# Reordering the first seven microseconds of a fused SSM and GEGLU kernel: tile 0 ahead of tile 1 through LayerNorm, other load requests, dummy matmuls between transposes

## Chip, cores and metric

One NeuronCore of a Trainium2 chip. The metric is the device time of one execution in microseconds, the median of several runs. Positions inside an execution are counted from the start of the profiled span, which is about 1.8 us shorter than the device time.

## The reference, cut to what matters

The input x is 2048 tokens of 512 features in bf16. It is normalised, and two branches read the result: a diagonal complex state-space layer (A) and a GEGLU feed-forward (B).

```python
def reference(A_x, ...):
    x = A_x
    xn = _layernorm(x, axis=-1)
    return x + _A_ref(xn, A_Lambda_re, A_Lambda_im, A_B_re, A_B_im, A_C_re, A_C_im, A_log_dt, A_Dskip) \
             + _B_ref(xn, B_w_gate, B_w_up, B_w_down)

def _B_ref(x, w_gate, w_up, w_down):
    return (_gelu(x @ w_gate) * (x @ w_up)) @ w_down      # 512 -> 1376 -> 512

def _A_ref(x, Lambda_re, Lambda_im, ..., log_dt, Dskip):  # cut
    dt = jnp.exp(log_dt)
    Lam_bar = jnp.exp(dt * (Lambda_re + 1j * Lambda_im))  # h = Lam_bar * h + Bu, token after token
    ...
```

Three small inputs of 1 KB each, `log_dt`, `Lambda_re` and `Lambda_im`, decide the recurrence.

## The kernel before

The kernel records each operation with its reads and writes; a scheduler of its own orders those of VectorE (DVE), ScalarE (ACT) and GpSimd (POOL) and gives every cross-engine dependence a semaphore. TensorE (PE) and the sync queue run in the order in which the program records them. The tokens are cut into 4 blocks of 4 tiles of 128. Per block the matmuls are gate and up (GU), Bu of the state-space branch (BU) and the output (DN). What starts the kernel, cut:

```python
# loads: sync queue, but w_gate's first chunk and the parameters on ScalarE's queue
for j in range(4):
    ld_x0(j)                                                  # tile j of block 0, 128 KB each
ld_w(WG, WGc, ins["B_w_gate"], 0, "scalar").nb = 900.0        # first 384 columns; nb: not before, in the scheduler's model
ld_w(WU, WUc, ins["B_w_up"], 0)                               # ... then chunks 1 of w_gate and w_up
for q, nm in enumerate(("A_log_dt", "A_Lambda_re", "A_Lambda_im")):
    S.dma(lambda e, q=q, nm=nm: e.dma_start(PROW.ap[4 * q:4 * q + 4, :], ins[nm]...), 1024, ..., queue="scalar")
# then on the sync queue: block 1 of x, transposing loads of B_re and B_im, more weights (load_B)

def params():                          # all three parameters, transposed by one small matmul
    PE(f, 100, PROWq + [IDN], [BANK[bank]], "Tpar")           # waits for all three loads
    ...                                # the tables of sines follow from it on POOL, DVE and ACT

def LN(b, js, on_act):                 # cut: statistics and aggregate per tile, then ONE root and reciprocal for all js
    ...
def GU_first(fts, early, banks):       # block 0, in PE's order (early = row blocks 0 to 2)
    for n in (1, 0):                   # tile 0's gate half, by halves of its transpose
        for ft in early: mm(ft, 0, 0, 1, [2 * n, 2 * n + 1], 2, 1, [XT0h[n]])
    for ft in early: mm(ft, 1, 0, 1)   # tile 0's up half
    params()                           # <-- the small transpose stands HERE in PE's order
    for ft in early:
        for u in range(2): mm(ft, u, 1, 2)                    # tile 1's gate and up
    ...                                # the rest: tiles 0 and 1, then the transposes of tiles 2 and 3, then tiles 2 and 3

PE(fwarm, ...)                         # 11 dummy matmuls of 512 columns
LN(0, [0, 1], True)
TR0(0, "AV"); TR0(1, "V", ...)         # PE transposes; copies of tile 0 half on ACT, half on DVE
LN(0, [2, 3], True, ...)
load_B()
GU_first(range(5), range(3), hbanks)
```

Of the kernel before, what the change touches and what calls it, by code (L numbers as in the profile page):

```python
# [15 lines left out]
SELF_LAT = 40.0  # L16
LAT = lambda d, op: SYNC_LAT if d.kind == "dma" or d.eng != op.eng else (0.0 if d.eng == "tensor" else SELF_LAT)
DMA_ISSUE = 500.0
# [43 lines left out]
class Op:  # L62
    __slots__ = ("id", "eng", "fn", "dur", "deps", "kind", "reads", "writes", "start", "finish",
                 "sem", "val", "users", "tag", "issue", "nb")

    def __init__(self, id_, eng, fn, dur, kind, reads, writes, tag):
        self.id, self.eng, self.fn, self.dur, self.kind = id_, eng, fn, float(dur), kind
        self.reads, self.writes, self.tag = reads, writes, tag
        self.deps, self.users = [], []
        self.start = self.finish = None  # L70
        self.sem = None
        self.val = None
        self.issue = DMA_ISSUE
        self.nb = 0.0


class Sched:
# [43 lines left out]
    def dma(self, fn, nbytes, reads=(), writes=(), tag="", after=(), is_output=False, queue="sync", issue=DMA_ISSUE):  # L121
        op = self._add(queue, fn, 2000.0 + nbytes / 0.30e3, "dma", reads, writes, tag, after)
        op.issue = issue
        if is_output:
            self.out_ops.append(op)
        return op

# [84 lines left out]
    def _forward(self, prio):  # L212
# [16 lines left out]
        while nleft:  # L229
# [36 lines left out]
            if op.kind == "dma":  # L266
                free_at[e] = st + op.issue
                xfer = op.dur - 2000.0
                t0 = max(st, dma_pipe)
                dma_pipe = t0 + xfer  # L270
                op.finish = t0 + xfer + 2000.0
            else:
                op.finish = st + op.dur
                free_at[e] = op.finish
# [8 lines left out]
    def emit(self):  # L283
# [19 lines left out]
        for e in ENGINES:  # L303
            seen = {}
            prog = []
            for op in order[e]:
                need = {}
                for d in op.deps:
                    if d.kind == "eng" and d.eng == e and e == "tensor":
                        continue  # L310
                    key = ("e", d.eng) if d.kind == "eng" else ("d", d.id)
                    if seen.get(key, 0) >= d.val:
                        continue
                    if key not in need or need[key].val < d.val:
                        need[key] = d
                for key, d in need.items():
                    seen[key] = d.val
                waits = [(d.sem, d.val) for d in need.values()]
                nwait += len(waits)
                prog.append((waits, op))  # L320
            plan[e] = prog
# [43 lines left out]
def build(nc, ins, out):  # L365
    with ExitStack() as es:
# [103 lines left out]
        def ld_x0(j):  # L470
            S.dma(lambda e, j=j: e.dma_start(X[j].ap, x2[128 * j:128 * (j + 1), :]), 128 * 1024, writes=[X[j]], tag="ld_x0")
        for j in range(4):
            ld_x0(j)
        ld_w(WG, WGc, ins["B_w_gate"], 0, "scalar").nb = 900.0
        ld_w(WU, WUc, ins["B_w_up"], 0)
        ld_w(WG, WGc, ins["B_w_gate"], 1)
        ld_w(WU, WUc, ins["B_w_up"], 1)
        for q, nm in enumerate(("A_log_dt", "A_Lambda_re", "A_Lambda_im")):
            S.dma(lambda e, q=q, nm=nm: e.dma_start(PROW.ap[4 * q:4 * q + 4, :], ins[nm].rearrange("(s p) -> s p", p=128)),
                  1024, writes=[PROWq[q]], tag="ld_" + nm, queue="scalar")  # L480
        def late_loads():
# [37 lines left out]
        SCR = A.alloc("SCR", [1], F32)  # L519
        ACT(lambda e: e.activation(SCR.ap, HALF.ap[:, 0:1], ACTF.Sqrt), 200, [HALF], [SCR], "sqrt0").nb = 1900.0  # L520
        POOL(lambda e: e.memset(HR.ap, 0.0), 300, [], HRp, "hr0")
# [61 lines left out]

        def tables_dve():
            for s in range(KP):
# [3 lines left out]
                  d_dve_1x(512), [IOTJ, W16p[0], K1s[s]], [F1s[s]], "f1")  # L589
            V(lambda e: e.tensor_scalar(A1.ap.bitcast(I32), F1.ap.bitcast(I32), 0x7FFFFFFF, None, ALU.bitwise_and), d_dve_ts4x(2048) * 2, F1s, [A1], "a1")  # L590

        def tables_act(after_gelu):
            t = ACT(lambda e: e.activation(SC16.ap, FRC.ap, ACTF.Sin, scale=SIN_SCALE), d_act(16) + 1300, [FRC], [SC16], "sin16", after=after_gelu)
            t = ACT(lambda e: e.activation(COST.ap, A1.ap, ACTF.Sin, bias=HPI.ap, scale=-SIN_SCALE), d_act(2048), [A1, HPI], [COST], "cost", after=[t])
            return ACT(lambda e: e.activation(SINT.ap, F1.ap, ACTF.Sin, scale=-SIN_SCALE), d_act(2048), [F1], [SINT], "sint", after=[t])

        def LN(b, js=range(4), on_act=False, after=()):
# [8 lines left out]
            if on_act:  # L606
                ACT(lambda e: e.activation(qb.ap, mv.ap[:, :, 1], ACTF.Sqrt, bias=EPS.ap), d_act(4), [mv, EPS, SCR], [qb], "sqrt")  # L607
            else:
                V(lambda e: e.tensor_scalar(sbq.ap, mv.ap[:, :, 1], EPS_BF16, None, ALU.add), D_TINY, [mv], [sbq], "sbq")
                POOL(lambda e: e.tensor_tensor(qb.ap, sbq.ap, HALF.ap[:, 0:j1 - j0], ALU.pow), 1100, [sbq, HALF], [qb], "pow")  # L610
            V(lambda e: e.reciprocal(rq.ap, qb.ap), 150, [qb], [rq], "rq")  # L611
            for j in js:
                tt = 4 * b + j
                xs = XN[tt % 8]
                V(lambda e, tt=tt, j=j, xs=xs: e.tensor_scalar(  # L615
                    xs.ap, X[tt].ap, mn.ap[:, j - j0:j - j0 + 1], rq.ap[:, j - j0:j - j0 + 1], ALU.subtract, ALU.mult),
                  d_dve_ts4x(512), [X[tt], mn, rq], [xs], "ln_n")

# [33 lines left out]
        def TR(b):  # L652
            tts = list(range(4 * b, 4 * b + 4))
            for j, tt in enumerate(tts):
                S.dma(lambda e, b=b, j=j, tt=tt: e.dma_start_transpose(
                    XNT[b].ap[:, :, 128 * j:128 * (j + 1)], XN[tt % 8].ap),
                    1.2 * 128 * 1024, reads=[XN[tt % 8]], writes=[XTk[b][j]], tag="tr_x%d" % b)

# [60 lines left out]
        def GU_first(fts, early, banks):  # L719

            def mm(ft, u, j0, j1, dks=range(KD), first=0, last=KD - 1, toks=None):
                W, Wc = ((WG, WGc), (WU, WUc))[u]
# [3 lines left out]
                def f(e):  # L726
                    ins_ = None
                    for dk in dks:
                        ins_ = e.matmul(PS[bank][:, q0:q0 + 128 * (j1 - j0)], W.ap[:, dk, 128 * ft:128 * (ft + 1)],  # L729
                                        XNT[0].ap[:, dk, 128 * j0:128 * j1], start=(dk == first), stop=(dk == last))  # L730
                    return ins_
                PE(f, d_pe([128 * (j1 - j0)] * len(dks)), [Wc[wchunk(ft)]] + (toks or XT0[j0:j1]), [BANK[bank]], "GU0")

            def evac(ft, h, after=()):
# [3 lines left out]
                                        d_act(256), [BANK[bank]], [GG[kk]], "gelu", after)  # L738
                ACT(lambda e: e.activation(UPB[kk].ap[:, 0:256], PS[bank][:, 256:512], ACTF.Copy),
                    d_act(256), [BANK[bank]], [UPB[kk]], "evU")  # L740
                V(lambda e: e.tensor_tensor(HTt[0][ft].ap[:, c0:c0 + 256], GG[kk].ap[:, 0:256], UPB[kk].ap[:, 0:256], ALU.mult),
                  d_dve_tt2x(256), [GG[kk], UPB[kk]], [HTt[0][ft]], "hmul")

            for n in (1, 0):
                for ft in early:
                    mm(ft, 0, 0, 1, [2 * n, 2 * n + 1], 2, 1, [XT0h[n]])
            for ft in early:
                mm(ft, 1, 0, 1)
            params()
            for ft in early:  # L750
                for u in range(2):
                    mm(ft, u, 1, 2)
            late = [ft for ft in fts if ft not in early]
            mm(late[0], 0, 0, 2)
            TR0(2, "V")
            TR0(3, "A")
            for ft in early:
                evac(ft, 0, [GATE["evTA"]])
            for ft in late[1:]:
                mm(ft, 0, 0, 2)  # L760
            for ft in late:
# [68 lines left out]
        def DN(b, split=False, tail=None):  # L830
# [38 lines left out]
            if split:  # L869
                for j in range(4):  # L870
                    seed(j); hidden(j)
                for j in range(4):
                    states(j); store(j)
            else:
                for j in range(4):
                    parts = ((0, D),) if tail is None or j < 3 else ((0, tail), (tail, D))
                    for c in parts:
                        seed(j, *c)
                    for c in parts:
                        hidden(j, *c); states(j, *c); store(j, *c)  # L880

        nwarm = 11
        wrm4 = WRM.ap.unsqueeze(1).broadcast_to([128, 4, 128])
# [14 lines left out]

        PE(fwarm, d_pe([512] * nwarm) * 1.6, [WRM], [BANK[wb]], "warm")
        LN(0, [0, 1], True)  # L900
        TR0(0, "AV")
        hbanks = [{ft: next_bank() for ft in range(5)} for h in range(2)]
# [3 lines left out]
        GU_first(range(5), range(3), hbanks)  # L906
        tables_dve()
        GATE["before_gelu"] = [tables_act([GATE["last_gelu"]])]
# [82 lines left out]
```

## Time and profile before

| | before |
|---|---|
| device time, median of 6 runs | 179.58 us (179.39 to 180.47) |
| profiled span | 177.6 us |
| PE busy | 173.5 us, 98% of the span |
| first gate matmul | 6.45 us |
| first Bu matmul | 16.1 us |

Part 1 of the page of the kernel before (busy us of each engine, its share of the span, and its instructions):

```profile
PE 173.5 (98%) x927; PEld 86.4 (49%) x927; DVE 156.3 (88%) x275; ACT 91.5 (52%) x175; POOL 10.1 (6%) x20
```

The chain that ended last, of the kernel before, in order of time (start, length, what):

```profile
5.11 0.42 DVE arena L615
...
5.58 0.41 PE PS L640 x4
...
6.45 0.83 PE PS L729 x12
...
7.30 0.84 PE PS L729 x12
8.15 0.11 PE PS L537
8.26 1.88 PE PS L729 x28
...
16.26 6.91 PE PS L667 x32
...
142.44 32.91 PE PS L846 x171
```

From 8.15 us on every piece is PE, and each begins where the last ends: PE has no pause to the end. So the time can fall in front of that point alone. The line of 6.45 us (12 gate matmuls) and that of 7.30 us (12 up matmuls) do not join: the last gate matmul starts at 7.06 us, and the first up matmul waits for the first chunk of w_up, which landed at 7.26. L615 and L640 are the normalising and the transposes. (The chain counts a matmul from the end of the one before it, so its starts lie up to 0.2 us behind those of the timeline: the first Bu matmul is at 16.26 here and at 16.10 there. Tables and text give the timeline's starts unless they speak of the chain.)

The timeline of the kernel before (start, length, engine, line, operation, output<-input, count; in brackets the idle time before and what ended it; ACTq and SPq are requests of loads):

```profile
1.60 0.42 ACTq L467 DMA_DIRECT2D arena<-in_B_w_gate_dram  x1
...
2.13 0.34 ACTq L479 DMA_DIRECT2D arena<-in_A_Lambda_im_dram  x1
...
4.87 6.94 SPq L489 DMA_TRANSPOSE arena<-in_A_B_re_dram  x1
5.11 0.74 DVE L615 TENSOR_SCALAR arena<-arena 128x512 bf16<-128x512 bf16 x2
...
7.30 0.67 PEld L729 LDWEIGHTS PS<-arena 128*128 128x128 bf16 x12 [0.20 <-DMA arena<-in_B_w_up_dram]
...
8.08 0.18 PE L537 MATMUL PS<-arena 12*128 12x12 bf16 x1
```

Lambda_im is asked for at 2.13 us, and the parameter transpose (L537) runs at 8.08 us. The trace's semaphore record, from which every landing time in this text is read, has Lambda_im landed at 5.58 us.

### The profile page before, as it was taken

What the parts mean: (1) busy time and instruction counts of PE and PEld (TensorE: products, weight loads), DVE (VectorE), ACT (ScalarE), POOL (GpSimd) and SP (SyncE); (2) the same over time, 40 slices, a digit from 0 to 9 for tenths busy, and PEclk for the clock granted to TensorE, in tenths of its full rate; (3) what the DMA queues carried; (4) which work ended last, traced back from release to release, by engine and by line L of the source; (5) the groups of instructions that cost most, each with busy time, mean ns of one, the idle gap of its engine ahead of it and who ended that gap; (6) DMA issues with size and microseconds to landing.
All of it is one profiled execution on the core that took longest, in us unless ns stands there. A gap on an engine that the chain in (4) does not pass through costs nothing.

```text
span 177.6 us, 2525 instructions
## 1 busy us (share of the span) xinstructions
PE 173.5 (98%) x927; PEld 86.4 (49%) x927; DVE 156.3 (88%) x275; ACT 91.5 (52%) x175; POOL 10.1 (6%) x20
## 2 busy tenths in 40 slices
PE   7899999999999999999999999999999999999994
PEld 2597464444644444444644444444464444444453
DVE  5759997998998999779999999999999999999311
ACT  3289999976766899002576495000658700620000
POOL 3120025000000002400000000000000000000000
PEclk9999999999999999999999999999999999999999
DMA  4999914999043000001015000000001000002211
GB/s 132 336 302 163 327 26 95 194 159 339 13 86 61 4 0 0 0 30 63 30 33 113 3 6 0 30 30 30 30 4 30 0 0 0 0 0 78 73 50 39
DMA packets 26387, 12.90 MB, mean 73 GB/s; under 512 B 17704, under 2 KB 26376, under 8 KB 26376
## 3 DMA queue, kind: packets, MB, share of 16 engines
q1 hardware_dynamic: 25824, 12.36, 28.3%
q10 hardware_dynamic: 552, 0.40, 0.9%
q8 instruction: 7, 0.11, 0.3%
q14 instruction: 4, 0.03, 0.1%
HBM read 6.46 MB, written 2.10 MB: 48 GB/s over the span
## 4 chain that ended last, share of the span: by engine, by line
PE 95%; DVE 2%; DMA 1%; issue 0%; ACT 0%; ACTq 0%; DVEq 0%
PE PS L846 37%; PE PS L806 34%; PE PS L667 16%; PE PS L729 5%; PE PS L780 3%; DMA arena<-in_A_x_dram 1%; DVE arena L603 1%; PE PS L640 0%; DVE arena L615 0%; ACT arena L607 0%; DVE arena L649 0%; DVE arena L864 0%; DVE arena L604 0%; DVE arena L611 0%; PE PS L537 0%
## 5 line engine op out<-in xcount | busy, mean ns | idle before, releaser
L846 PE MATMUL PS<-arena 128*128 128x512 bf16 (+3 forms) x323 | 66.2, 366 | 0.0
L806 PE MATMUL PS<-arena 128*128 128x512 bf16 x280 | 61.7, 379 | 0.0
L846 PEld LDWEIGHTS PS<-arena 128*128 128x128 bf16 (+1 forms) x323 | 30.8, 98 | 35.2
L821 ACT ACTIVATE arena<-PS 128x512 bf16<-128x512 f32 x35 | 20.8, 598 | 46.4 <-PE PS L806 33.0
L806 PEld LDWEIGHTS PS<-arena 128*128 128x128 bf16 x280 | 27.3, 98 | 32.1
L700 DVE TENSOR_TENSOR_SCAN arena<-arena 128x512 bf16<-128x512 f32 x32 | 38.8, 1253 | 0.0
L667 PE MATMUL PS<-arena 128*128 128x512 bf16 x128 | 28.3, 379 | 0.0
L824 ACT ACTIVATE arena<-PS 128x512 bf16<-128x512 f32 x35 | 20.8, 597 | 4.9 <-PE PS L806 4.9
L667 PEld LDWEIGHTS PS<-arena 128*128 128x128 bf16 x128 | 12.5, 98 | 14.9
L864 DVE TENSOR_TENSOR arena<-PS,arena 128x512 bf16<-128x512 f32 (+2 forms) x17 | 10.9, 651 | 9.6 <-PE PS L846 9.6
L671 ACT ACTIVATE arena<-PS 128x512 bf16<-128x512 f32 x32 | 17.7, 597 | 3.0 <-PE PS L667 2.9
L826 DVE TENSOR_TENSOR arena<-arena 128x512 bf16<-128x512 bf16 x35 | 13.7, 416 | 2.9 <-ACT arena L824 2.9
L838 ACT ACTIVATE PS<-arena 128x512 f32<-128x512 bf16 (+2 forms) x17 | 9.6, 581 | 5.5 <-DVE arena L864 4.8
L603 DVE BATCH_NORM_STATS2 arena<-arena 128x6 f32<-128x512 bf16 x16 | 10.1, 680 | 1.2 <-DMA arena<-in_A_x_dram 1.1
L729 PE MATMUL PS<-arena 128*128 128x256 bf16 (+1 forms) x104 | 9.5, 248 | 0.2
L687 DVE TENSOR_TENSOR arena<-arena 128x4096 bf16<-128x4096 bf16 (+1 forms) x5 | 9.3, 1857 | 0.0
L689 DVE TENSOR_TENSOR arena<-arena 128x4096 bf16<-128x4096 bf16 (+1 forms) x5 | 9.3, 1856 | 0.0
L712 DVE TENSOR_TENSOR arena<-arena 128x4096 bf16<-128x4096 bf16 x4 | 9.1, 2286 | 0.0
L713 DVE TENSOR_TENSOR arena<-arena 128x4096 bf16<-128x4096 bf16 x4 | 9.1, 2286 | 0.0
L729 PEld LDWEIGHTS PS<-arena 128*128 128x128 bf16 x104 | 8.1, 98 | 1.1 <-issue 0.3
L622 DVE TENSOR_TENSOR arena<-arena 128x512 bf16<-128x512 bf16 x16 | 6.0, 414 | 0.0
L780 PE MATMUL PS<-arena 128*128 128x192 bf16 x64 | 5.9, 246 | 0.0
(84 smaller groups left out, 106.5 us busy)
## 6 DMA issues: line engine op xcount, KB each, us to landing
out_dram<-arena SPq DMA_DIRECT2D x15, 128.0 KB, 1.7
arena<-in_A_x_dram SPq DMA_DIRECT2D x3, 512.0 KB, 7.3
arena<-in_B_w_down_dram SPq DMA_DIRECT2D x1, 1280.0 KB, 6.9
arena<-in_A_x_dram SPq DMA_DIRECT2D x4, 128.0 KB, 3.0
arena<-in_B_w_gate_dram SPq DMA_DIRECT2D x1, 512.0 KB, 6.1
arena<-in_B_w_up_dram SPq DMA_DIRECT2D x1, 512.0 KB, 7.0
arena<-in_B_w_gate_dram SPq DMA_DIRECT2D x1, 480.0 KB, 4.4
arena<-in_B_w_up_dram SPq DMA_DIRECT2D x1, 480.0 KB, 5.6
```

What stands on the lines that cost most here:

```text
L603: V(lambda e, tt=tt: e.bn_stats(ST[tt].ap, X[tt].ap), d_dve_1x(512), [X[tt]], [ST[tt]], "bnst", after)
L667: ins_ = e.matmul(PS[bank][:, :], BBT[c][dk].ap[:, 128 * s:128 * (s + 1)], XNT[b].ap[:, dk, :], start=(dk == 0), stop=(dk == KD - 1))
L671: ACT(lambda e, bank=bank, k3=k3, s=s, c=c: e.activation(SSc[k3][s][c].ap, PS[bank][:, :], ACTF.Copy), d_act(512), [BANK[bank]], [SSc[k3][ ...
L700: V(lambda e, g=g, rb=rb, init=init: e.tensor_tensor_scan(g.ap, rb, g.ap, init, ALU.mult, ALU.add), d_dve_scan(512), [g, PA[RRr]] + ([CARc ...
L729: ins_ = e.matmul(PS[bank][:, q0:q0 + 128 * (j1 - j0)], W.ap[:, dk, 128 * ft:128 * (ft + 1)], XNT[0].ap[:, dk, 128 * j0:128 * j1], start=( ...
L780: ins_ = e.matmul(dst, XNT[b].ap[:, dk, 128 * j:128 * (j + 1)], WGU[:, :, dk, f0:f0 + m], start=(dk == 0), stop=(dk == KD - 1))
L806: ins_ = e.matmul(PS[bank][0:m, c0:c1], W.ap[:, dk, 128 * ft:128 * ft + m], XNT[b].ap[:, dk, c0:c1], start=(dk == 0), stop=(dk == KD - 1))
L821: GATE["last_gelu"] = ACT(lambda e, bg=bg, kk=kk, m=m: e.activation(GG[kk].ap[0:m, :], PS[bg][0:m, :], ACTF.Gelu_apprx_tanh), d_act(512), ...
L824: ACT(lambda e, bu=bu, kk=kk, m=m: e.activation(UPB[kk].ap[0:m, :], PS[bu][0:m, :], ACTF.Copy), d_act(512), [BANK[bu]], [UPB[kk]], "evU")
L826: V(lambda e, kk=kk, m=m, ft=ft, k2=k2: e.tensor_tensor(HTt[k2][ft].ap[0:m, :], GG[kk].ap[0:m, :], UPB[kk].ap[0:m, :], ALU.mult), d_dve_tt ...
L846: ins_ = e.matmul(PS[bank][:, c0:c1], l_[:, 128 * j:128 * (j + 1)], r_[:, c0:c1], start=False, stop=last and n == len(ops) - 1, skip_group ...
L864: V(lambda e: e.tensor_tensor(OUTB[ko].ap[:, c0:c1], PS[bank][:, c0:c1], XD[tt].ap[:, c0:c1], ALU.add), d_dve_1x(c1 - c0), [BANK[bank], XD ...
```

## The change

The intent is an earlier first matmul, and no pause behind it:

1. Tile 0 leads: `LN_first` takes tile 0's root and reciprocal under tile 1's statistics, with links that fix DVE's order without a semaphore wait. Both halves of tile 0's transpose are copied by ACT.
2. Three short dummies on PE between the transposes of tile 0 and tile 1, and 10 long ones in front instead of 11.
3. Loads: tiles 2 and 3 in one; w_gate asked for right behind tile 1's request (before Lambda_re); Lambda_re after w_gate, and Lambda_im after the roots of both tiles (its "not before" is 4800 in the scheduler's nanoseconds).
4. PE's order: tile 1's gate half in front of every up matmul; the up halves of tiles 0 and 1 in one matmul of 256 columns. The parameter transpose stands between. The gate halves of the two later row blocks now all stand in front of the transposes of tiles 2 and 3.
5. Smaller things off the first microseconds: two copies of up halves saved on ACT, the last block's order.

```diff
-        for j in range(4):
-            ld_x0(j)
-        ld_w(WG, WGc, ins["B_w_gate"], 0, "scalar").nb = 900.0
+        ld_x0(0)
+        ld_x0(1)
+        S.dma(lambda e: e.dma_start(X_all.ap[:, 2:4, :], x2[256:512, :].rearrange("(j p) d -> p j d", p=128)),
+              256 * 1024, writes=X[2:4], tag="ld_x0")
+        ld_w(WG, WGc, ins["B_w_gate"], 0, "scalar").nb = 550.0
...
-        for q, nm in enumerate(("A_log_dt", "A_Lambda_re", "A_Lambda_im")):
+        for q, (nm, nb) in enumerate((("A_log_dt", 0.0), ("A_Lambda_re", 600.0), ("A_Lambda_im", 4800.0))):
             S.dma(...
-                  1024, writes=[PROWq[q]], tag="ld_" + nm, queue="scalar")
+                  1024, writes=[PROWq[q]], tag="ld_" + nm, queue="scalar").nb = nb
...
+        def LN_first():          # cut: every DVE operation is linked behind the one before it
+            for step, j in ((stats, 0), (aggr, 0), (stats, 1), (recip, 0), (aggr, 1), (norm, 0), (recip, 1), (norm, 1)):
+                step(j)
...
-            for n in (1, 0):
+            for n in range(2):
                 for ft in early:
-                    mm(ft, 0, 0, 1, [2 * n, 2 * n + 1], 2, 1, [XT0h[n]])
+                    mm(ft, 0, 0, 1, [2 * n, 2 * n + 1], toks=[XT0h[n]])
             for ft in early:
-                mm(ft, 1, 0, 1)
+                mm(ft, 0, 1, 2)
             params()
             for ft in early:
-                for u in range(2):
-                    mm(ft, u, 1, 2)
+                mm(ft, 1, 0, 2)
...
-        nwarm = 11
+        nwarm = 10
...
-        LN(0, [0, 1], True)
-        TR0(0, "AV")
+        LN_first()
+        TR0(0, "AA")
+        fill(3)
```

The scheduler's model of DMA and of order-only links also changed; later in the kernel it only exchanges operations of DVE and ACT.

## The prediction

> **What bounds the kernel now.** TensorE. The page gives PE 173.5 of 177.6 us (98%); the chain of waits is PE without a pause from 8.15 to 175.37 us. The listed PE waits are 1.0 us (first memset) and 0.7 us (first normalised tile). Then the first up matmul starts at 7.30 where 7.05 was due: w_up's first chunk landed at 7.26. Only the first 7.3 us can be shortened; the 159 us from the first Bu matmul (16.1 us) on are matmul work that the change keeps.
>
> **The start, from the timeline.** Tile 0 lands at 2.85, tile 1 at 3.41. DVE does statistics 0 and 1 (0.61 each), both aggregates (to 4.38), ScalarE the root (4.50 to 4.79), DVE the reciprocal (to 4.99), normalise 0 (5.11 to 5.52), normalise 1 (to 5.84). Transposes start at 5.58; copies end at 6.28 and 6.30; the first gate matmul starts at 6.45.
>
> **What the change does, costed.**
> 1. Tile 0 goes ahead, its root under statistics 1. Estimate from these durations: root 0 3.9 to 4.2, reciprocal 0 to 4.46, normalise 0 4.63 to 5.04 (0.48 earlier); normalise 1 5.33 to 5.74 (only 0.1 earlier: own root and reciprocal).
> 2. Tile 0's transposes at 5.1, both copies (0.38 each) on ScalarE, done by 5.8 and 6.15. In PE's order the gate matmuls still stand behind tile 1's transposes (5.8 to 6.0). First gate matmul: about 6.05, 0.4 earlier.
> 3. Tile 1's gate half now precedes any up matmul. 24 gate matmuls of 128 columns (0.056 each) push the first need of w_up to about 7.45, behind its landing: the 0.25 us pause goes. Tile 1's copy (ready about 6.8) may cost 0.1. Merging 24 up matmuls of 128 columns into 12 of 256 (0.109) saves 0.04.
> 4. One sync-queue load fewer (0.46 us an issue) and w_gate 0.28 us earlier: weights and the transposed B behind them should land 0.2 to 0.4 earlier. B's first half landed at 15.42; it will be wanted at about 15.45, so it just fits. The Trainium skill ("DMA: Bandwidth & Descriptors", "Issuing engines are not separate DMA queues") says both queues interleave on the same engines; the trace agrees: tiles 2 and 3 landed only at 5.35 and 6.17 beside w_gate.
> 5. Smaller dummies, two up-copies fewer on ScalarE, the last block's order: off the path.
>
> Gain: 0.4 + 0.25 - 0.1 + 0.04, about 0.6 us (0.3%). It should survive: DVE's last chain ended at 160.4 for an estimated need at 161.2, and the last block's new order gives it 2.4 us more.
>
> **Predicted: 179.2 us, 178.6 to 180.0 in 8 of 10. Faster by over 2%: 1%; within 2%: 96%; slower by over 2%: 3%.**
>
> **Right or wrong in the profile.** Normalise 0 ends near 5.05; first gate matmul near 6.05; no wait for w_up; first Bu matmul near 15.45; PE's chain unbroken to about 174.7; tail as before.
>
> **What would make it wrong.** Lambda_im is now asked for on ScalarE's queue only after tile 1's root, at about 5.1 us, into full DMA engines. The parameter transpose, in PE's order at 7.45 us, waits for it. Before, it landed 3.1 us after its issue ended; if that repeats, PE stalls about 1 us and the gain is gone. If it queues behind the long B load (whose issue took 6.9 us), the loss is 4 us or more: my 3%. Smaller: tile 1 delayed by the earlier w_gate; B landing no earlier; ScalarE becoming a wait around 20 to 32 us.

## The result, and the profile after

| | before | after |
|---|---|---|
| device time, median of 6 runs | 179.58 us (179.39 to 180.47) | 180.65 us (180.22 to 180.98) |
| ratio to before (95% interval) | | 1.0051 (1.0027 to 1.0076) |
| profiled span | 177.6 us | 178.7 us |
| first gate matmul | 6.45 us | 6.30 us |
| parameter transpose | 8.08 us | 9.12 us |
| first Bu matmul | 16.1 us | 17.2 us |

A ratio here is the mean time of one kernel's fast runs over that of the other's of the same rounds, so it is not quite the ratio of the medians. The change costs about 0.9 us. It is within 2%, as predicted, but above the range of 178.6 to 180.0.

PE's waits after (what waited, for what: us in total, times, longest):

```profile
PE PS L547 <- DMA arena<-in_A_Lambda_im_dram: 1.3, 1, 1.3
PE PS L937 <- DVE arena L525: 1.0, 1, 1.0
PE PS L768 <- DMA arena<-in_B_w_gate_dram: 0.2, 1, 0.2
```

The chain that ended last, after:

```profile
4.66 4.32 DMA arena<-in_A_Lambda_im_dram
8.98 0.14 issue
9.12 0.16 PE PS L547
9.28 2.29 PE PS L768 x20
...
17.32 6.91 PE PS L706 x32
...
143.50 32.91 PE PS L887 x171
```

Its first pieces are no longer PE's. It goes back from the parameter transpose (L547) to a DMA of 1 KB that was under way from 4.66 to 8.98 us. The timeline after shows why it was asked for so late, and that the parts in front of it did what they should:

```profile
1.32 0.40 ACTq L475 DMA_DIRECT2D arena<-in_B_w_gate_dram  x1
...
4.58 0.43 DVE L628 TENSOR_SCALAR arena<-arena 128x512 bf16<-128x512 bf16 x1
...
4.66 0.26 ACTq L489 DMA_DIRECT2D arena<-in_A_Lambda_im_dram  x1
...
5.00 6.75 SPq L499 DMA_TRANSPOSE arena<-in_A_B_re_dram  x1
...
6.30 1.51 PE L768 MATMUL PS<-arena 128*128 128x128 bf16 x24 [0.18 <-DMA arena<-in_B_w_gate_dram]
...
9.12 0.16 PE L547 MATMUL PS<-arena 12*128 12x12 bf16 x1 [1.30 <-DMA arena<-in_A_Lambda_im_dram]
```

Normalise 0 (L628) starts at 4.58 us for 5.11 before. The first gate matmul is 0.15 us earlier, and no up matmul waits for w_up. Then PE stands 1.3 us at the transpose. From the first Bu matmul on, the two kernels take the same time: the run of Bu, gate, up and output pieces ends 159.1 us behind its start in both (16.26 to 175.35, and 17.32 to 176.41).

### The profile page after: what moved, and what is told of

It is laid out like the page before. It is cut to its first block, busy times and chain, and to the rows that moved or that the text cites. A ratio compares the mean times of both kernels' runs of the same rounds, so it can differ in the third digit from the quotient of the medians.

```text
span 178.7 us, 2518 instructions
## 1 busy us (share of the span) xinstructions
PE 173.9 (97%) x917; PEld 86.5 (48%) x917; DVE 157.1 (88%) x275; ACT 91.5 (51%) x175; POOL 10.2 (6%) x21
## 4 chain that ended last, share of the span: by engine, by line
PE 94%; DMA 4%; DVE 1%; issue 0%; ACT 0%
PE PS L887 37%; PE PS L847 34%; PE PS L706 15%; PE PS L768 4%; PE PS L821 3%; DMA arena<-in_A_Lambda_im_dram 2%; DMA arena<-in_A_x_dram 1%; DVE arena L616 1%; PE PS L679 0%; DVE arena L619 0%; DVE arena L905 0%; PE PS L547 0%; DVE arena L625 0%; ACT arena L621 0%
## 5 line engine op out<-in xcount | busy, mean ns | idle before, releaser
L862 ACT ACTIVATE arena<-PS 128x512 bf16<-128x512 f32 x35 | 21.1, 603 | 35.3 <-PE PS L847 34.5
L865 ACT ACTIVATE arena<-PS 128x512 bf16<-128x512 f32 x35 | 21.2, 605 | 5.9 <-PE PS L847 5.8
L710 ACT ACTIVATE arena<-PS 128x512 bf16<-128x512 f32 x32 | 17.8, 597 | 2.0 <-PE PS L706 2.0
L639 DVE BATCH_NORM_STATS2 arena<-arena 128x6 f32<-128x512 bf16 x14 | 8.9, 680 | 0.1
L589 DVE SCALAR_TENSOR_TENSOR arena<-arena 128x512 bf16<-128x512 bf16 x8 | 5.5, 744 | 0.8 <-ACT arena L586 0.8
```

Source lines behind the costliest of these rows:

```text
L710: ACT(lambda e, bank=bank, k3=k3, s=s, c=c: e.activation(SSc[k3][s][c].ap, PS[bank][:, :], ACTF.Copy), d_act(512), [BANK[bank]], [SSc[k3][ ...
L862: GATE["last_gelu"] = ACT(lambda e, bg=bg, kk=kk, m=m: e.activation(GG[kk].ap[0:m, :], PS[bg][0:m, :], ACTF.Gelu_apprx_tanh), d_act(512), ...
L865: ACT(lambda e, bu=bu, kk=kk, m=m: e.activation(UPB[kk].ap[0:m, :], PS[bu][0:m, :], ACTF.Copy), d_act(512), [BANK[bu]], [UPB[kk]], "evU")
```

## The experiments

Theory A is that the whole loss is this one wait: the request for Lambda_im, moved to 4.66 us, lands too late for a transpose that stands fixed in PE's order. Rival B is that the earlier start is eaten by something else, the weights landing later or DVE and ACT falling behind, so that without this wait another one would come. In all kernels below where an order is said to be moved, it was moved in the finished schedule, so that nothing else changes place, unless the text says otherwise. They ran in three sets, each on one chip with its own runs of the kernel before: the first four below, the next four, the last four. One of that kernel's runs (310 us) is not counted.

| run | what it is | median us | ratio to before (95%) |
|---|---|---|---|
| e1_im_early | after, Lambda_im asked for early | 178.88 | 0.9978 (0.9965 to 0.9990) |
| e2_before_im_late | before, Lambda_im asked for late | 180.65 | 1.0078 (1.0062 to 1.0094) |
| e3_par_later | after, transpose later in PE's order | 180.07 | 1.0035 (1.0023 to 1.0047) |
| e4_no_lead | e1 without tile 0's lead | 179.44 | 1.0002 (0.9988 to 1.0015) |
| e7_quiet | after, little queued (one look) | 179.58 | |
| e8_par_later2 | e3, mended | 179.27 | 0.9992 (0.9980 to 1.0004) |
| e5_loads_undone | e1 with the old loads | 179.38 | 0.9994 (0.9981 to 1.0006) |
| e6_dummies_undone | e1 with the old dummies | 179.02 | 0.9982 (0.9967 to 0.9997) |
| e11_im_early_again | e1 once more | 179.11 | 0.9980 (0.9967 to 0.9993) |
| e12_loads_undone_again | e5 beside e1 | 179.21 | 0.9985 (0.9973 to 0.9998) |
| e10_up_first | e1 with the old order of up | 179.60 | 1.0013 (0.9999 to 1.0027) |
| e9_short_warm | e1 with fewer dummies | 180.66 | 1.0049 (1.0018 to 1.0080) |

### e1_im_early: only the request is moved back

```diff
         S.schedule()
+        q = S.order["scalar"]
+        op = next(o for o in q if o.tag == "ld_A_Lambda_im")
+        q.remove(op)
+        q.insert(1 + max(i for i, o in enumerate(q) if o.tag == "ld_A_Lambda_re"), op)
```

> The changed kernel, with one move: the request for Lambda_im goes from behind the two roots on ScalarE's queue to directly behind Lambda_re; no other instruction moves on any engine. Theory A (the loss is TensorE standing at the parameter transpose until Lambda_im lands): Lambda_im lands before 6.6 us instead of 8.98, the 1.3 us wait is gone, the first Bu matmul comes at about 15.8 us instead of 17.2, and the time is 179.1 us, 0.3% under the kernel before. Rival B (the weights now land later, w_gate 6.26 for 5.81 and w_up 7.60 for 7.26, or ScalarE and DVE fall behind, and the wait at the transpose only covers that): another wait of about 1 us takes its place, and the time stays at 180.3 us or above.

Measured: 178.88 us, ratio 0.9978. Lambda_im was asked for at 2.19 us and landed at 5.92; the transpose started at 7.80 and the first Bu matmul at 15.85 (the prediction had 15.45). The chain of e1_im_early:

```profile
0.99 4.45 PE PS L937 x10
5.44 0.43 PE PS L679 x4
5.86 0.32 PE PS L943 x3
6.18 0.32 PE PS L679 x4
6.50 1.36 PE PS L768 x24
7.87 0.11 PE PS L547
7.97 2.29 PE PS L768 x20
...
16.02 6.91 PE PS L706 x32
```

Moving one request of 1 KB turns the change from 0.5% slower to 0.2% faster. Rival B falls: there was no second wait behind the first. The chain also shows what bounds the start in this look: PE itself, whose 10 dummies (L937) and first transposes ran at half rate. In e11_im_early_again, the same kernel, the full rate came at 4.39 us and w_gate, landing at 6.38, held the first gate matmul instead.

### e2_before_im_late: the late request alone, on the kernel before

```diff
         S.schedule()
+        q = S.order["scalar"]
+        op = next(o for o in q if o.tag == "ld_A_Lambda_im")
+        q.remove(op)
+        q.insert(1 + min(i for i, o in enumerate(q) if o.tag == "sqrt"), op)
```

> The kernel before, with one move: the request for Lambda_im goes behind the first root on ScalarE's queue (issued at about 4.5 us instead of 2.1). Nothing else of the change. Theory A: it lands at 8.5 to 9 us, the parameter transpose that stood at 8.08 us waits 0.5 to 1 us, and the time is 180.1 to 180.6 us (ratio about 1.004). Rival B: within 0.1 us of the kernel before.

Measured: 180.65 us, ratio 1.0078; a larger loss than expected. PE's waits of e2_before_im_late, and its chain:

```profile
PE PS L537 <- DMA arena<-in_A_Lambda_im_dram: 1.6, 1, 1.6
```

```profile
4.54 5.40 DMA arena<-in_A_Lambda_im_dram
```

Asked for at 4.54, it landed at 9.94 us, 5.4 us later. (This look is its slowest run, 181.38 us.) The late request by itself costs the kernel before 0.0078 or 1.4 us, so nothing else of the change is needed for the loss.

### e3_par_later and e8_par_later2: the late request kept, the transpose moved

```diff
         S.schedule()
+        q = S.order["tensor"]          # e3 and e8: Tpar directly before the transposes of tile 2
+        op = next(o for o in q if o.tag == "Tpar")
+        q.remove(op)
+        q.insert(min(i for i, o in enumerate(q) if o.tag == "T0" and o.reads[0].name == "XN2"), op)
+        q = S.order["vector"]          # e3 and e8: its two readers behind the normalising of tiles 2 and 3
+        i = next(i for i, o in enumerate(q) if o.tag == "par")
+        j = max(i for i, o in enumerate(q[:40]) if o.tag == "ln_n")
+        q[i:j + 1] = q[i + 2:j + 1] + q[i:i + 2]
+        j = [i for i, o in enumerate(q) if o.tag == "evT"][1]          # e8 alone: tile 2's copy right behind "par"
+        q.insert(1 + next(i for i, o in enumerate(q) if o.tag == "par"), q.pop(j))
```

> The changed kernel with the late request kept, but the parameter transpose moved in TensorE's order behind the up matmuls and late gates (20 matmuls of 256 columns), directly before the transposes of tiles 2 and 3; on DVE its two readers go behind the normalising of tiles 2 and 3. Theory A: Lambda_im still lands near 9 us, the transpose now stands at about 9.8 us and waits for nothing, first Bu matmul at about 15.8 us, time 179.1 to 179.3 us. Rival B: time stays at 180.3 us or above.

Measured: 180.07 us, worse than expected. Lambda_im landed at 9.15 us and the transpose, at 9.94, waited for nothing. My edit had made another wait. PE's waits of e3_par_later:

```profile
PE PS L768 <- DVE arena L688: 0.7, 1, 0.7
```

L688 is the copy of tile 2's transpose. On DVE it stood behind two small operations that need a power from POOL (L550, 1.0 us), and that power could start only behind the moved transpose. An engine that runs in order hands one late input on to all that stands behind it.

> e3_par_later mended: there the parameter transpose no longer waited for Lambda_im, but on DVE the copy of tile 2 stood behind two small parameter operations that wait for a 1.0 us power on GpSimd, and TensorE waited 0.74 us for that copy. Here that copy goes in front of them; the late request is kept. Theory A: no TensorE wait for Lambda_im nor for the copy, first Bu matmul at about 15.9 us, 178.9 to 179.2 us, equal to e1_im_early within 0.2 us. If another part of the change were to blame for the loss, it would stay at 180 us.

Measured: 179.27 us, ratio 0.9992. Lambda_im landed at 9.00 us, as late as in the changed kernel, and no PE wait names it. The timeline of e8_par_later2:

```profile
10.26 0.18 PE L547 MATMUL PS<-arena 12*128 12x12 bf16 x1
```

So it is not the late landing that costs, but its meeting a fixed place in PE's order. It is 0.0014 or 0.25 us above e1_im_early, a little more than the 0.2 expected, but on another chip; in its look PE paused about 0.3 us for w_gate's second chunk (landed at 9.23), which the late gate matmuls now reach sooner. (The looks of this second set lack some 2% of the matmul records, so I read no fine chain from them; the first Bu matmul on record is at 16.3 us, with one missing in front of it.)

### e7_quiet: why a 1 KB load takes 4.3 us

```diff
         S.schedule()
+        root = [o for o in S.order["scalar"] if o.tag == "sqrt"][1]
+        [o for o in S.order["sync"] if o.tag == "ld_w"][1].deps.append(root)
```

> A measurement, not a candidate: the changed kernel with its late request for Lambda_im (issued at about 4.7 us), but on the sync queue every load behind w_up's first chunk is held until the second root is done (about 5 us). So when Lambda_im is asked for, little stands queued before the DMA engines. Theory A (the 1 KB waits behind the loads asked for before it): issue to landing shrinks from 4.3 us (4.66 to 8.98) to about 2 us, so it lands near 7 us. Rival C (a late request by itself takes that long, whatever is queued): it lands at 8.5 us or later all the same. The weights land later, so the kernel's time says nothing.

Measured: asked for at 4.68 us, it landed at 6.86 us: 2.2 us, against 4.3 us in the changed kernel, and the transpose no longer waited. The timeline of e7_quiet:

```profile
4.68 0.26 ACTq L489 DMA_DIRECT2D arena<-in_A_Lambda_im_dram  x1
...
7.90 0.18 PE L547 MATMUL PS<-arena 12*128 12x12 bf16 x1
```

Rival C falls (one look, but the four with a full queue, after, e2, e3 and e8, took 4.3 to 5.4 us). The packets show where the time goes. The DMA queues of the changed kernel from 6 to 7.8 us (packets, MB, share of 16 engines, where over 100% means only that the packets' times add up to more than the window; q1 is the sync queue, q10 ScalarE's):

```profile
q1 hardware_dynamic: 652, 0.60, 106.1%
```

There is no line for q10: ScalarE's queue moved nothing. The next 0.9 us of the same kernel, with the same columns:

```profile
q1 hardware_dynamic: 346, 0.34, 108.3%
q10 hardware_dynamic: 8, 0.00, 0.8%
```

And the DMA queues of e7_quiet from 5.9 to 6.8 us:

```profile
q1 hardware_dynamic: 203, 0.16, 95.6%
q10 hardware_dynamic: 8, 0.00, 0.8%
```

Lambda_im has 8 packets: four of 256 bytes and their four completions. In the changed kernel the request was issued by 4.93 us, and ScalarE's queue had moved its last packet of the other loads by 5.73; yet for two more microseconds only the sync queue moved. The first packet of Lambda_im started at 7.88 us. In e7_quiet it started at 5.94. So the request was held up by the traffic of the sync queue, although it was on another queue and alone there. It did not wait for all of it: it landed ahead of w_up's second chunk (10.57) and block 1 of x (12.06), whose requests had begun earlier. Nor does e7_quiet single out the loads in front of it: the long request for the transposing load of B_re, which begins at 5.00 us in the changed kernel, right behind that for Lambda_im, begins at 6.51 here, behind its first packet. Whether the earlier loads or this request held it, and at which stage it stood, the traces do not show.

### e4_no_lead and e10_up_first: what the two useful parts are worth

```diff
-        LN_first()                 # e4: on e1_im_early
+        LN(0, [0, 1], True)
```

> e1_im_early with the lead of tile 0 undone: both tiles go through LN together as in the kernel before (one root, one reciprocal for both). What the order-only links are worth by themselves. If they are worth what I predicted (0.4 us at the first gate matmul), the first gate matmul goes from about 6.3 to 6.7 us and the time is 0.3 to 0.4 us above e1_im_early. Rival: the first gate matmul stands behind w_gate (landed at 6.26 us in the changed kernel) and tile 1, which gained only 0.1 us, so the lead is worth at most 0.15 us.

Measured: 179.44 us, ratio 1.0002, which is 0.0024 or 0.43 us above e1_im_early on the same chip. The first gate matmul moved from 6.34 to 6.57 us. The prediction's size for the lead (0.4 us) agrees with the time, though the two intervals just touch; the looks show half of it, but what holds the first gate matmul differs between looks too (PE's half rate, w_gate's landing).

```diff
             for ft in early:       # e10: on e1_im_early
-                mm(ft, 0, 1, 2)
+                mm(ft, 1, 0, 1)
             params()
             for ft in early:
-                mm(ft, 1, 0, 2)
+                mm(ft, 0, 1, 2); mm(ft, 1, 1, 2)
```

> e1_im_early with TensorE's order of the first block undone: tile 0's up matmuls again in front of tile 1's gate half, tile 1's gate and up after the parameter transpose, 128 columns each (the scheduler then also shuffles small DVE operations later, which have slack). What the new order is worth. I predicted 0.25 us for the wait that it removes: with the first gate matmul at about 6.35 us the up matmuls are wanted at 7.0 us, w_up lands at about 7.4, so TensorE should wait about 0.4 us there and the time be 0.3 to 0.5 us above the yardstick. If the order is worth nothing: within 0.1 us.

Measured: 179.60 us, ratio 1.0013, 0.0033 or 0.6 us above e1_im_early_again beside it. PE's waits of e10_up_first:

```profile
PE PS L768 <- DMA arena<-in_B_w_up_dram: 0.5, 1, 0.5
PE PS L679 <- DVE arena L628: 0.3, 1, 0.3
```

Its first gate matmul came at 6.04 us, the earliest of all, and PE then waited for w_up until 7.41. The other wait, for the first normalised tile, is in e11_im_early_again too (0.2 us). Here the scheduler also exchanged small operations of DVE and ACT later; PE shows no wait there, and its chain from the first Bu piece on is 159.1 us as in the others.

**The two parts pay only together, as far as these runs go.** Without the lead, the rest of e1_im_early is level with the kernel before (1.0002), and with the lead but the old order also (1.0013, interval from 0.9999). The first half has its trace: in e10_up_first the earlier start only waits longer for w_up. Why the new order alone (e4_no_lead) does not show the 0.25 us that the prediction gave it is not shown; in its look the first gate matmul came at 6.57 us, later than before the change (6.45).

### e5_loads_undone, e12_loads_undone_again, e11_im_early_again: the load part

```diff
-        ld_x0(0)                   # on e1_im_early
-        ld_x0(1)
-        S.dma(... x2[256:512, :] ...)
+        for j in range(4):
+            ld_x0(j)
...                                 # and ScalarE's queue: log_dt, Lambda_re, w_gate, Lambda_im
```

> e1_im_early with the loads asked for as before the change: tiles 0 to 3 in four loads, w_gate behind Lambda_re. My prediction gave the load part 0.2 to 0.4 us earlier landings. If so, w_up lands near 7.8 us, TensorE waits for it, and the time is 0.2 us above e1_im_early. Rival: the profile of the changed kernel shows w_gate and w_up landing later than before (6.25 for 5.81, 7.60 for 7.26), so the load part is worth nothing or costs: w_gate at 5.8, w_up near 7.4, time within 0.1 us of e1_im_early.

Measured: 179.38 us, ratio 0.9994, on another chip than e1_im_early (0.9978), so the two were run again side by side, with nothing changed in either:

> e1_im_early again, unchanged, as the yardstick on this chip for the three runs beside it: 178.9 us, ratio 0.998 to the kernel before. If the first result was chance, it comes out at 1.000.

> e5_loads_undone again, now beside e1_im_early on one chip. The first time the two ran on different chips (0.9994 and 0.9978 to the kernel before). If the load part is worth the 0.2 us that I predicted, it is again about 0.0015 slower than the yardstick; if the difference was between chips, the two agree within 0.0005.

Measured: 179.11 us (0.9980) and 179.21 us (0.9985). The first result of e1_im_early is confirmed; the load part is worth 0.0005 with overlapping intervals, so nothing that these runs resolve. Its landings moved the wrong way, if at all. In the four looks with the old loads (before, e2, e5, e12) w_gate landed at 5.52 to 5.81 us and w_up at 7.07 to 7.55. In the nine with the new loads and the usual traffic, w_gate landed at 5.39 to 6.38 (median 6.23; seven of the nine later than 5.81) and w_up at 7.31 to 7.63.

### e6_dummies_undone and e9_short_warm: the dummies

```diff
-        nwarm = 10                 # on e1_im_early
+        nwarm = 11                 # e6; e9: 8
...
-        fill(3)                    # e6 and e9: none
```

> e1_im_early with the dummies as before: 11 long ones and none between the transposes. In e1_im_early all 10 ran at 0.427 us each (half rate) and ended just as tile 0 was ready, and the chain of waits goes through them. An eleventh moves tile 0's transposes from 5.23 to about 5.65 us; without the three small ones tile 1's follow at once (to about 6.5 us at half rate). Expected: first gate matmul 6.5 us for 6.34, time 0.1 to 0.2 us above e1_im_early. If the dummies between the transposes hold the clock up, the loss is larger (the gate matmuls would run at 0.107 us).

Measured: 179.02 us, ratio 0.9982, within noise of e1_im_early (0.9978, 0.9980). The expected 0.1 to 0.2 us was not seen in the times, although in the look the first gate matmul was indeed at 6.64 us; that look was its slowest run, 179.55 us.

> e1_im_early with 8 long dummies for 10 and none between the transposes: an attempt to beat it. Where the clock is still at half rate, 10 dummies end at 5.23 us, 0.1 us after tile 0 is ready, and the three small ones cost 0.32 us in the chain. With 8 the first gate matmul should come at about 6.2 us (behind tile 1's transposes), 0.1 to 0.15 us under the yardstick, 178.75 us. If the dummies are what brings the full clock in time, it comes later, the 24 gate matmuls take 0.107 us each, and the time is up to 1 us above.

Measured: 180.66 us, ratio 1.0049, the second of the expected cases. PE's timeline in e9_short_warm:

```profile
0.99 3.59 PE L937 MATMUL PS<-arena 128*128 128x512 bf16 x8 [0.99 <-DVE arena L525]
5.20 1.21 PE L679 MATMUL PS<-arena 128*128 128x128 bf16 x8 [0.62 <-DVE arena L628]
6.20 2.77 PE L768 MATMUL PS<-arena 128*128 128x128 bf16 x24
8.90 0.19 PE L547 MATMUL PS<-arena 12*128 12x12 bf16 x1
```

The 24 gate matmuls start at 6.20, earlier than in e1_im_early (6.34), but take 2.77 us instead of 1.53: PE stays at half rate up to 10.1 us. One of its six runs took 179.00 us; that the full rate came in time there is a guess, which no look shows. The Trainium skill ("TensorE: Matmul & The Clock Gate", "Why this matters for your kernels") asks for at least 4 us of continuous work to reach the full rate. This look fits: 8 dummies keep PE busy for 3.59 us, with 0.6 us of idle time behind them, where 10 at half rate take about 4.4 us. It is no proof: the kernel before had the full rate 2.7 us after its first dummy.

**The version that beats both kernels is e1_im_early**: 178.88 and 179.11 us, ratios 0.9978 and 0.9980 on two chips, both intervals under 1. e6_dummies_undone and e12_loads_undone_again, which lack one of its parts, are level with it. The changed kernel stands at 1.0051.

## Why the prediction was wrong

- **The bound (right).** PE without a pause to the end, only the first microseconds can change: the chain from the first Bu piece on took 159.1 us in both kernels and in every look whose matmul record is complete enough to tell, so these kernels differ by what happens in front of it. No new wait of PE came later, as predicted.
- **Tile 0's lead (right).** Normalise 0 was predicted to end at 5.04 us and ended at 5.02; leaving it out costs 0.43 us in e4_no_lead.
- **First gate matmul "about 6.05, 0.4 earlier" (0.15 us).** It started at 6.30: w_gate landed only at 6.25, and PE stood 0.18 us for it. Step 4 of the prediction failed here: "weights and the transposed B behind them should land 0.2 to 0.4 earlier". The request was 0.28 us earlier, the landing 0.45 later. B's first half came earlier (14.07 for 15.42), but that is not the load part's doing as far as the runs show: it landed at 14.15 in e2 with the old loads and at 15.49 in e11 with the new ones, and PE did not wait for it in either kernel. Step 5 ("Smaller dummies ... off the path") failed as well: normalise 0 was done at 5.02 us, but the transposes of tile 0 started at 5.22, behind dummies at half rate. In the one look where the full rate (4.24) and w_gate (5.64) both came early, e10_up_first, the first gate matmul stood at 6.04, as predicted.
- **The wait for w_up (right).** Gone; putting it back costs 0.6 us with the earlier start (e10_up_first), where 0.25 was predicted; by itself the gain was not seen (e4_no_lead).
- **The step that failed.** The gain "0.4 + 0.25 - 0.1 + 0.04, about 0.6 us" has no term for Lambda_im. It counts on all three parameters being there when PE reaches the transpose at about 7.45 us. The prediction saw the risk, and priced it from the kernel before ("it landed 3.1 us after its issue ended; if that repeats, PE stalls about 1 us and the gain is gone"), but left it out of the sum and of the middle of the range. It should have been the expected case: the request goes out when 16 DMA engines are full. It measured 4.05 us from the end of its issue (4.93 to 8.98) and a stall of 1.3 us. That the risk was priced near the truth (about 1 us) is partly luck: the request went out 0.4 us earlier than supposed (4.66 for 5.1) and took 0.9 us longer than the 3.1. The observed change, +0.9 us by ratio, is what the rest of the change gains less this stall: e1_im_early, which has no such wait, shows -0.4 us (0.6 was predicted), and the difference between the two, 0.0073 of 179.5 us, is 1.3 us.
- **The page of the skill that step 4 rested on.** "DMA: Bandwidth & Descriptors", section "Issuing engines are not separate DMA queues", says that DMAs of all issuing engines end up on the same 16 engines and interleave. I used this for the size of the weights' landings, and did not apply it to the 1 KB request. The same page, section "Queues, rings and completion order", says that each DMA engine "round-robins between the queue rows it has work for, at *packet* granularity". From that alone a lone request on its own queue should be served after a packet or so. Measured, its first packet started 2.95 us after its issue ended, and 1 us after in e7_quiet, where the sync queue had less given to it. That does not refute the page, which speaks of queue rows that an engine has work for: the traces do not show when the request came to stand in its row. For what a late request costs, the measurement decides.
- **The fallback of 4 us (did not come).** The request did not have to wait for the transposing load of B_re (issue over at 11.75 us): it landed at 8.98.

Open: at which stage the small request stands behind the other queue, whether the loads before it or the request for B_re right behind it hold it, and why w_gate mostly lands later when it is asked for earlier.

## What to carry to other kernels

On an engine that runs in order, a tiny operation that joins several inputs is only as early as the latest of them: before moving a request later "because nobody needs it yet", look up where its first reader stands in that order, and take as its latency what a request of the same moment took in full traffic, not what an early one took. Ask for kilobyte-sized inputs before the megabytes, even on another queue. When two improvements sit in series in front of one arrival (an earlier start, and an order that needs that arrival later), test them together: each alone may show nothing.

## What the Trainium skill lacked or had wrong

- "DMA: Bandwidth & Descriptors", "Queues, rings and completion order": packet-wise round robin between queues does not by itself predict the latency of a small request. A 1 KB load alone on ScalarE's queue took 4.3 to 5.4 us from request to landing (changed kernel, e2) behind a full sync queue, and 2.2 us when less was queued (e7_quiet). No page that I read says how long a small request waits beside another queue's loads.
- "TensorE: Matmul & The Clock Gate", "Part 1: The HAM clock gate": it puts the full rate around 4 us into sustained activity, "±500ns run-to-run", and adds that the number of slow matmuls varies. Its two rates agree with the traces (dummies of 512 columns 0.427 us apart, then 0.216). The spread was wider here: with 10 or 11 dummies from 0.99 us on, the trace's clock record has the full rate at 3.73 us (before), 5.20 (after) and 6.89 (e6), that is 2.7 to 5.9 us after the first dummy; in e9, with 8, at 10.1 us.
